# A fused attention and feed-forward kernel: one order of work exchanged for another, with the two banks of a PSUM tile counted as one

## The chip, the cores and the metric

The kernel runs on one core of a Trainium2 chip. The metric is device time in microseconds (us) of one execution. The core has five engines with instruction queues of their own: PE (matrix products), DVE and ACT and POOL (elementwise work), and SP, which here only issues DMA transfers. Each engine takes its instructions strictly in the order in which they are written; engines wait for one another through semaphores. Products land in PSUM, which has eight banks of 512 fp32 columns per partition.

## The reference

Eight batches of linear attention with a cosine weighting are followed by a feed-forward layer with leaky ReLU:

```python
def phi(x, c, s):
    r = np.maximum(x, 0.0)
    return np.concatenate([r * c, r * s], axis=-1)
q_p = phi(q, cos_w, sin_w)                     # q, k, v: (8, 8, 576, 64)
k_p = phi(k, cos_w, sin_w)
kv  = np.einsum('bhsf,bhsd->bhfd', k_p, v)
z   = np.sum(k_p, axis=2)
num = np.einsum('bhsf,bhfd->bhsd', q_p, kv)
den = np.einsum('bhsf,bhf->bhs', q_p, z)[..., None] + 1e-06
x = (num / den) as 4608 tokens x 512           # then:
h = x @ w_in                                   # 512 x 2048
g = np.maximum(0.01 * h, h)
out = g @ w_out                                # 2048 x 512
```

Inputs and output are fp32; the kernel computes in fp16 with fp32 sums.

## The kernel before

**Groups.** The 4608 tokens are nine groups of 512: group g < 8 is the first 512 tokens of batch g, group 8 the 64 last tokens of all eight batches. A number behind a step's name is its batch or group.

**Steps.** Loads are `Lq`, `Lk`, `Lv` (an ending a or b is half the heads, n the tail of 64 tokens), `Lw1`, `Lw2`; all go through SP's queue in their order, into four staging buffers that are used in turn (`stage`), so a load can start only when the casts that read the buffer's earlier content are done. `q1.0.c`, `k2.3.s` and the like are relu times cosine or sine into `qp` and `kp`; `cw2` casts a quarter of w_out (four quarters, two halves each: `cw2.2.0` is needed for hidden blocks 8 and 9 of 16). `K` sums kp times v into PSUM, `kv` copies it out; `T` (by PE, with copy `tc`) or `Tq` (by DMA) transposes q; `N` multiplies q with kv; `D` divides (three DVE instructions); `X` with `xc` (by PE) or `Tx` (by DMA) transposes the result into `xT`.

**Feed-forward.** Group 0 takes the plain route: `M` is its first product and `a` the leaky ReLU, `E` its second product (E3.7: hidden blocks 14 and 15 of 16, token quarter 3) and `ec` the copy out. Group 1's first product is `H` with `ha`. From then on products go as seven instead of eight block products with sums between: `P` is the first product of groups 2 to 8 and `F` the second of groups 1 to 8; `Ws`, `Xs`, `Tw`, `S` are the operand sums (DVE); `b s u y z` and `t r` the sums between products, `a c e d` the ReLUs; `st` stores.

**PSUM.** Eight banks are four pairs: `h0`, `h1`, `o`, `n`. The pair `n` is one tile of two banks for the whole kernel, `h0` and `h1` are one tile each until the step `split.h` (near F1.6) makes each two tiles, `o` is two tiles from the start. Semaphores are set by tile: a product that writes one bank of a tile waits for every reader of that tile that stands ahead of it in the order, and a reader on one engine waits for an earlier reader of the same tile on another. E2 and E3 use the two banks of `n`, as do the transposes X2.0 to X2.3 and every `N`.

**What sets the order.** Nothing in the file decides it: the string `ORDER` (from line 17 on) names some 1500 steps one after the other, with a letter for the engine where there is a choice (D is DVE, A is ACT, P is POOL), and the loop at the file's end issues them so. `idle` steps are PE products of zeros. In the order before, the second cast of w_out's third quarter stands on POOL, E3.7 stands behind the copy `ec2:D`, and the copies of X2 are `xc2.0:D xc2.1:A xc2.3:A xc2.2:D`.

Of the kernel before, what the change touches and what calls it, by code (L numbers as in the profile page):

```python
# [31 lines left out]
M10.1 kp1.0.c:D a5 q1.1.c:D M12.0 M4.1 M13.1 M12.1 q1.2.c:P M15.0 M15.1 M14.0 a2 a6 M14.1 cw2.1.1:D kp1.1.s:D
a7 E3.0 Lv1a k1b.8.c:D kp1.3.s:D E2.0 E1.0 cw2.1.0:A T1.0 Lk4n E0.0 E2.1 E1.1 E0.1 E2.2 tc1.0:A q1.2.s:A T1.1
kp1.2.s:D Lv1b q1.3.s:P E2.3 tc1.1:A k1b.5.c:A k1b.0.c:P E1.2 T1.2 v1.0:P tc1.2:D T1.3 E3.1 tc1.3:D k1b.6.c:D
k1b.1.c:P v1.1:A Lv2n K1a k1b.3.c:D Lw2.2 k1b.7.c:A kv1a:A k1b.2.c:D k1b.4.c:P E1.3 N1a.0 E0.2 Lw2.3 E3.2
N1a.1 D1a.0 v1.3:P D1a.1 v1.2:A E3.3 Lq2 K1b kv1b:D E0.3 cw2.2.0:P X1a.0 X1a.1 xc1a.1:D N1b.0 E1.4 xc1a.0:A
N1b.1 D1b.0 E2.4 E0.4 cw2.2.1:P X1b.0 Lk2n cw2.3.0:P xc1b.0:A D1b.1 E1.5 Tw1.0:D Tw2.0:D E0.5 Lk2 Ws1.1:D Lv2
X1b.1 xc1b.1:A H0.0 Ws1.2:D E2.5 H1.0 Ws0.2:D H2.0 H2.1 H3.0 E0.6 q2.1.c:D H1.1 H0.1 ha0 E3.4 q2.1.s:D E2.6
cw2.3.1:P H3.1 E2.7 H5.0 ha1 Tw3.0:D q2.0.s:A H5.1 E0.7 ec0:A H4.0 q2.0.c:A Ws1.4:D E1.6 H4.1 q2.2.s:P ha2
k2.4.s:D Lq3 q2.3.c:D st0.0 H6.0 q2.3.s:D E3.5 q2.2.c:P k2.0.s:A H7.0 Tw1.1:D H6.1 H7.1 H8.0 Tw2.1:D k2.3.s:P  # L40
# [11 lines left out]
k4.4.c:P P2.2.1 F1.4.0.0 N3.1 c2.1 b2.2:A P2.2.5 q4.0.s:A F1.4.0.1 P2.1.4 st0.2 s2.2:A D3.1 d2.1 S2.1l:D
q4.3.c:P F1.3.0.0 N3.2 P2.2.2 D3.2 st0.3 P2.2.6 F1.3.0.1 k4.0.c:P u2.2:A P2.2.3 P2.2.7 Lk5n F1.4.1.0 k4.2.s:D
k4.1.c:A q4.0.c:D Lq5 N3.3 k4.1.s:P a2.2 z2.2:D k4.3.s:A P2.3.1 D3.3 e2.2 F1.3.1.0 v4.0:P F1.3.1.1 v4.1:P
b2.3:A P2.3.5 P2.3.6 k4.3.c:A k4.2.c:A y2.2:D F1.4.1.1 u2.3:A k4.0.s:A st1.2 c2.2 P2.3.2 s2.3:D Tx3 r1.4:D
P2.2.4 r1.3:D P2.3.3 P2.3.7 K4 a2.3 d2.2 z2.3:D e2.3 y2.3:D P2.3.4 q4.2.c:P S2.2l:D F2.1.0.0 d2.3 F2.6.0.0
kv4:D F2.1.0.1 F2.1.1.0 F2.1.1.1 c2.3 S2.1h:D P3.0.1 k5.4.s:P Xs3.1:D Xs3.2:D b3.0:A Tq4.0 P3.0.5 Xs3.3:D
S2.2h:D Tq4.1 P3.1.1 S2.3l:D s3.0:A Xs3.4:D P3.0.6 u3.0:A t1.2:A P3.0.2 q5.3.s:P Lk5 q5.0.s:P F2.6.0.1 P3.0.7
F2.6.1.0 z3.0:D P3.0.3 a3.0 y3.0:D F2.6.1.1 N4.0 P3.1.5 F2.2.0.0 e3.0 b3.1:A P3.1.2 D4.0 t2.2:D st1.5 Lv5
q5.0.c:A S2.3h:D q5.1.c:A P3.1.6 N4.1 s3.1:A P3.0.4 Lv5n F2.2.0.1 Lq6 q5.2.s:P a3.1 F2.2.1.0 D4.1 d3.0 P3.1.3  # L60
P3.2.1 u3.1:A z3.1:D P3.2.5 F2.7.0.0 F2.7.0.1 e3.1 N4.2 q5.1.s:D P3.1.7 c3.0 F2.2.1.1 D4.2 b3.2:A y3.1:D
F2.7.1.0 st1.4 F2.7.1.1 S2.4l:D s3.2:A P3.2.6 P3.2.2 u3.2:D c3.1 t3.2:D P3.1.4 k5.2.s:P N4.3 k5.3.s:D P3.2.3
a3.2 P3.2.7 r2.2:A d3.1 z3.2:D k5.0.s:A F2.4.0.0 F2.4.0.1 F2.5.0.0 P3.3.5 y3.2:D k5.2.c:P e3.2 q5.3.c:P P3.3.1
k5.1.c:A D4.3 b3.3:A S2.4h:D P3.2.4 Tq5.0 Tx4 F2.5.0.1 P3.3.6 F2.5.1.0 s3.3:A q5.2.c:D k5.1.s:D F2.5.1.1 c3.2
k5.0.c:P F2.4.1.0 u3.3:A d3.2 P3.3.7 F2.4.1.1 r2.5:D P3.3.3 P3.3.2 v5.1:A v5.0:A k5.3.c:A F2.3.0.0 st1.3
k5.4.c:D F2.3.0.1 y3.3:D r2.4:D c3.3 P3.3.4 F2.3.1.0 F3.1.0.0 F2.3.1.1 z3.3:D e3.3 d3.3 K5 q6.0.s:D q6.1.c:D
Lk6 Lk6n a3.3 Lv6 S3.1h:D F3.1.0.1 P4.0.1 S3.1l:D b4.0:A Xs4.1:D S3.2l:D P4.1.1 P4.0.5 Xs4.2:D st2.5 S3.2h:D
kv5:A P4.0.6 Xs4.3:D Xs4.4:D u4.0:A r2.3:D P4.0.2 s4.0:A a4.0 F3.1.1.0 P4.0.7 N5.0 S3.3h:D P4.0.3 F3.6.0.0
z4.0:D F3.6.0.1 e4.0 st2.2 P4.1.5 F3.1.1.1 q6.0.c:D k6.4.s:P F3.6.1.0 b4.1:A Tq5.1 y4.0:D F3.6.1.1 s4.1:A
t1.3:A D5.0 P4.1.6 u4.1:A st2.4 P4.1.3 N5.1 P4.0.4 P4.1.7 F3.2.0.0 S3.3l:D t2.3:D c4.0 z4.1:D d4.0 F3.2.0.1  # L70
q6.1.s:A D5.1 y4.1:D k6.0.s:P k6.2.c:D F3.2.1.0 P4.1.2 k6.0.c:A F3.7.0.0 P4.2.1 F3.2.1.1 Lv6n e4.1 a4.1 P4.2.5
F3.7.0.1 b4.2:D r3.2:D s4.2:A P4.2.6 P4.2.2 k6.2.s:P S3.4h:D P4.1.4 k6.4.c:A q6.2.c:P q6.3.s:D q6.2.s:P
F3.5.0.0 u4.2:D N5.2 F3.7.1.0 q6.3.c:P k6.3.c:A D5.2 d4.1 c4.1 a4.2 Lq7 F3.7.1.1 Tq6.0 F3.5.0.1 P4.3.1 v6.1:A
N5.3 P4.2.7 t3.3:D F3.5.1.0 F3.4.0.0 z4.2:D v6.0:A D5.3 P4.2.3 Tx5 Lv7n P4.3.5 y4.2:D F3.4.0.1 k6.1.c:D
k6.1.s:A e4.2 F3.5.1.1 Lk7n st2.3 F3.4.1.0 b4.3:A P4.3.6 k6.3.s:D c4.2 s4.3:D P4.2.4 u4.3:A F3.4.1.1 S3.4l:D
P4.3.7 r3.5:D S4.1l:D K6 d4.2 y4.3:D q7.0.c:P P4.3.2 S4.2l:D F3.3.0.0 kv6:A P4.3.4 z4.3:D Xs5.1:D c4.3 N6.0
P4.3.3 Xs5.3:D Xs5.2:D d4.3 Tq6.1 F3.3.0.1 Lk7 e4.3 F3.3.1.0 r3.4:D P5.0.1 P5.1.1 q7.1.c:P a4.3 Lt0.0 P5.0.5
F3.3.1.1 b5.0:D s5.0:A D6.0 P5.0.6 P5.0.2 P5.0.3 F4.1.0.0 q7.0.s:A st3.2 r3.3:D S4.1h:D N6.1 u5.0:A P5.0.7
a5.0 Xs5.4:D S4.2h:D P5.1.5 z5.0:D y5.0:D F4.1.0.1 e5.0 k7.4.s:P k7.4.c:A F4.1.1.0 F4.6.0.0 b5.1:D F4.6.0.1
k7.1.c:P s5.1:A Lv7 q7.1.s:D F4.6.1.0 P5.0.4 P5.1.2 P5.1.6 c5.0 q7.3.s:D P5.1.3 D6.1 F4.1.1.1 q7.3.c:D  # L80
F4.6.1.1 d5.0 u5.1:A a5.1 t1.4:A z5.1:D P5.1.7 S4.3l:D P5.2.1 F4.2.0.0 Tq7.0 st3.5 P5.2.5 y5.1:D N6.2 F4.2.0.1
F4.2.1.0 t2.4:D e5.1 F4.2.1.1 P5.1.4 F4.7.0.0 b5.2:A D6.2 k7.3.c:A s5.2:D P5.2.6 q7.2.s:A S4.3h:D N6.3 Lt0.1
r4.2:A P5.2.2 P5.2.3 F4.5.0.0 u5.2:A d5.1 k7.2.s:D a5.2 F4.7.0.1 z5.2:D P5.3.1 e5.2 b5.3:A F4.7.1.0 st3.4
P5.2.7 D6.3 c5.1 F4.7.1.1 st3.3 F4.5.0.1 k7.1.s:D k7.0.s:A y5.2:D Tx6 t3.4:D P5.3.5 k7.0.c:A P5.3.6 P5.3.2
S4.4l:D v7.1:D q7.2.c:D k7.2.c:A u5.3:A s5.3:D k7.3.s:A F4.5.1.0 F4.4.0.0 c5.2 v7.0:P P5.2.4 z5.3:D F4.5.1.1
d5.2 Lt1.0 K7 r4.5:D S4.4h:D P5.3.7 Xs6.1:D P5.3.3 y5.3:D Xs6.3:D F4.3.0.0 a5.3 Xs6.2:D F4.4.0.1 F4.4.1.0
# [894 lines left out]
```

## Time and profile before

| | |
|---|---|
| median of 3 runs | 275.84 us (275.52 to 275.86) |
| the profiled execution's own time | 275.22 us |
| its span, from first to last instruction | 273.4 us |
| PE / PE's weight loads busy | 264.4 / 223.9 us |
| DVE / ACT / POOL busy | 215.2 / 179.3 / 104.4 us |
| HBM read / written | 36.70 / 9.44 MB |
| TensorE clock granted | 0.996 |

A row of the profile's timeline has the start, the duration, the engine, the line in the file, the operation with its output and inputs (buffer numbers left out), how many instructions are merged in it, and in brackets how long the engine sat idle before it and what it waited for. A product's duration in these rows (0.59 us for a first one of 512 columns) is longer than the distance to the next one, since products are pipelined; the distance is what counts for PE's time.

### The profile page before, as it was taken

Reading aid. Unit: us, or ns where it says so; the run is one execution under the profiler, and the core shown is the slowest. Engines: PE = TensorE matmul, PEld = TensorE weight load, DVE = VectorE, ACT = ScalarE, POOL = GpSimd, SP = SyncE. Lnnn points to the kernel's source line nnn. Section 1 sums busy time; section 2 is a strip of 40 time slices with the busy share of each in tenths; the row PEclk is TensorE's granted clock in tenths of the full one; section 3 lists DMA queues with packets and bytes.
Section 4 is the critical chain, followed back from the end, with each engine's and each line's share of the span. In section 5 each row is a group of like instructions: output and inputs, shape, how many; then the busy total and the mean of one; then the engine's idle time right before and its main releaser. Section 6 shows DMA issues by size and latency. Waiting matters only on the chain.

```text
span 273.4 us, 6788 instructions
## 1 busy us (share of the span) xinstructions
PE 264.4 (97%) x2734; PEld 223.9 (82%) x2734; DVE 215.2 (79%) x429; ACT 179.3 (66%) x306; POOL 104.4 (38%) x76
## 2 busy tenths in 40 slices
...
GB/s 236 357 395 384 400 330 353 344 267 272 319 187 349 218 178 262 345 187 260 262 200 168 168 336 207 154 191 78 120 63 131 80 93 61 40 79 0 41 134 97
DMA packets 87631, 57.06 MB, mean 209 GB/s; under 512 B 53808, under 2 KB 82480, under 8 KB 87088
## 3 DMA queue, kind: packets, MB, share of 16 engines
...
q10 hardware_dynamic: 608, 0.52, 0.6%
...
HBM read 36.70 MB, written 9.44 MB: 169 GB/s over the span
## 4 chain that ended last, share of the span: by engine, by line
PE 82%; DMA 10%; DVE 4%; SPq 1%; issue 1%; ACT 1%; POOL 0%; ACTq 0%
PE o L869 32%; PE h L783 32%; DMA stage<-in_moe_w_out_dram 7%; PE h L685 5%; PE n L558 3%; PE n L470 3%; DMA stage<-in_k_dram 2%; PE n L707 1%; PE o L707 1%; PE h L869 1%; PE n L869 1%; DVE xs L582 1%; DVE kp L431 1%; SPq L321 1%; PE o L374 0%
## 5 line engine op out<-in xcount | busy, mean ns | idle before, releaser
L869 PEld LDWEIGHTS <-g 128*128 128x128 f16 x640 | 61.8, 98 | 6.5
L869 PE MATMUL o<-w,g 128*128 128x256 f16 x480 | 64.7, 273 | 0.0
L803 ACT ACTIVATE g<-h 128x512 f16<-128x512 f32 x84 | 48.4, 600 | 24.0 <-PE h L783 12.7
L783 PEld LDWEIGHTS <-w 128*128 128x128 f16 x448 | 48.2, 114 | 1.4 <-issue 0.5
L783 PE MATMUL h<-xT,w 128*128 128x256 f16 x336 | 48.9, 273 | 0.3 <-ACT xT L234 0.3
L783 PEld LDWEIGHTS <-wext 128*128 128x128 f16 x336 | 36.5, 114 | 0.7 <-issue 0.2
L869 PE MATMUL o<-T,ext 128*128 128x256 f16 x224 | 31.6, 273 | 0.0
L242 POOL TENSOR_SCALAR qp<-stage,cos_t 128x512 f16<-128x512 f32 (+1 forms) x12 | 26.1, 2176 | 13.6 <-DMA stage<-in_q_dram 6.6
L242 POOL TENSOR_SCALAR kp<-stage,sin_t 128x512 f16<-128x512 f32 (+1 forms) x12 | 21.3, 1777 | 23.8 <-DMA stage<-in_k_dram 13.8
L869 PEld LDWEIGHTS <-ext 128*128 128x128 f16 x256 | 24.9, 98 | 2.6
L230 DVE TENSOR_TENSOR h<-h,u 128x512 f32<-128x512 f32 x28 | 19.5, 695 | 9.1 <-PE h L783 3.9
L783 PE MATMUL h<-X,wext 128*128 128x256 f16 x176 | 25.4, 272 | 0.0
L230 DVE TENSOR_TENSOR y<-h,s 128x512 f32<-128x512 f32 x28 | 19.2, 685 | 4.4 <-PE h L783 3.3
L242 POOL TENSOR_SCALAR kp<-stage,cos_t 128x128 f16<-128x128 f32 (+2 forms) x13 | 18.6, 1434 | 9.7 <-DMA stage<-in_k_dram 9.7
L582 DVE TENSOR_TENSOR xs<-n,rden 128x512 f16<-128x512 f32 x30 | 20.7, 692 | 1.0
L242 POOL TENSOR_SCALAR qp<-stage,sin_t 128x512 f16<-128x512 f32 (+1 forms) x9 | 19.1, 2126 | 6.2 <-DMA qpT<-qp 5.3
L234 ACT COPY h<-h 128x512 f32<-128x512 f32 x24 | 13.8, 574 | 9.9 <-PE h L783 9.5
L803 ACT ACTIVATE g<-y 128x512 f16<-128x512 f32 x28 | 17.7, 632 | 1.7 <-DVE y L230 1.7
L869 PE MATMUL o<-ext,g 128*128 128x256 f16 x128 | 18.2, 272 | 0.0
L230 DVE TENSOR_TENSOR osb<-o,ext 128x512 f32<-128x512 f32 x22 | 15.0, 686 | 2.5 <-PE o L869 1.7
L234 ACT COPY u<-h 128x512 f32<-128x512 f32 x21 | 12.3, 586 | 7.0 <-PE h L783 6.9
L783 PE MATMUL h<-X,w 128*128 128x256 f16 x112 | 16.9, 273 | 0.0
...
## 6 DMA issues: line engine op xcount, KB each, us to landing
...
```

Source lines behind the costliest of these rows:

```text
L230: eng.tensor_tensor(out=o, in0=a, in1=b, op=how)
L234: nc.scalar.copy(o, i)
L242: eng.tensor_scalar(out=o, in0=i, scalar1=0.0, scalar2=col, op0=ALU.max, op1=ALU.mult)
L321: nc.sync.dma_start(w2_st(i), w2v[i])
L470: nc.tensor.matmul(ps[:, h // NC, (h % NC) * NE : (h % NC + 1) * NE], lhsT=kps[sl, s, :], rhs=vms[sl, s, :], start=start, stop=stop, skip_ ...
L558: nc.tensor.matmul(pairs["n"][lo:hi, h // 4, (h % 4) * NE : (h % 4 + 1) * NE], lhsT=qpT[j // 2][:, j % 2, h, lo:hi], rhs=kv[b][:, h, :],)
L582: nc.vector.tensor_tensor(out=o, in0=ps[:, :, 0 : 4 * NE].rearrange("p a (b e) -> p a b e", e=NE)[:, :, :, 0:D], in1=r.rearrange("p (a b) ...
L685: nc.tensor.matmul(ps[:, m % 2], lhsT=w1[m // 4, c // 2][:, c % 2, m % 4 : 512 : 4], rhs=xT[1][:, :, c, :], start=(c == 0), stop=(c == NKC ...
L707: nc.tensor.matmul(bank[4 + tt], lhsT=G[0][:, m, tt * P : (tt + 1) * P], rhs=w2[:, m, :], start=(m == 0), stop=(m == NFT - 1),)
L783: nc.tensor.matmul(ps[:, mi * HT : (mi + 1) * HT], lhsT=a[:, c, 2 * r0 + mi : 512 : 4], rhs=b[:, c], start=(n in (1, 5) and mi == 0 and c ...
L803: nc.scalar.activation(G[g % 2][:, m : m + 2, r * HT : (r + 1) * HT], {"a": A, "c": y22, "e": E, "d": B_}[e].rearrange("p (m t) -> p m t", ...
L869: nc.tensor.matmul(ps[:, tt], lhsT=a[:, i, tt * P : (tt + 1) * P], rhs=b[:, i], start=(first and i == 0 and (apart or tt == 0)), stop=(i = ...
```

## The change

Only the string `ORDER` differs. Up to `M1.1.1 N0b.1 D0b.1 idle.5.1.5`, that is through the loads and attention of the first batch, it is the same; from there to the end the same steps stand in another order, and some on another engine (of the steps with a letter or a fixed engine, DVE has 357 in place of 352, ACT 293 in place of 301, POOL 68 in place of 65). The new order was made by a planner, which is not in the file, that treats the two banks of one PSUM tile as one resource. PE's instructions are the same in number and kind.

```diff
-M1.1.0 M1.1.1 N0b.1 D0b.1 idle.5.1.5 X0b.0 M2.0.0 M3.0.0 xc0b.0:A M3.0.1 M3.1.0 M2.0.1 Lq1 X0b.1 q1.0.s:D M5.0
+M1.1.0 M1.1.1 N0b.1 D0b.1 idle.5.1.5 M2.0.0 M2.0.1 M3.0.0 X0b.0 M3.0.1 xc0b.0:D M2.1.0 M2.1.1 M3.1.0 X0b.1
...
-E1.7 k2.2.s:A k2.2.c:D H9.0 Ws0.4:D H9.1 E3.6 H8.1 Tq2.1 k2.3.c:P ec2:D k2.4.c:D k2.1.c:D ec1:A ha3 k2.1.s:D
-E3.7 Tq2.0 k2.0.c:D H11.0 H10.0 H10.1 ha4 H11.1 H13.0 Lk3 S1.1l:D H12.0 S1.3l:D v2.0:D Ws0.3:D ha5 Tw4.1:D
+q2.2.s:D E3.5 q2.0.s:D q2.0.c:D q2.2.c:D E3.6 H0.1 H1.0 H1.1 H2.0 Tw2.0:D H2.1 ha0 Lq3 H3.0 H3.1 k2.3.c:D E3.7
+H4.0 q2.3.s:P Lv2 Ws0.2:D ec2:D k2.3.s:A Tw4.0:D k2.2.c:P Lv2n H4.1 ha1 H6.0 H5.0 Tq2.0 ec1:D H6.1 H5.1 ha2
...
-r1.2:A F1.7.0.0 N2.3 k3.0.c:P D2.3 st0.1 F1.7.0.1 F1.5.0.0 F1.7.1.0 S1.4l:D X2.1 Tq3.0 v3.0:D X2.0 Tq3.1
-k3.3.s:A X2.2 X2.3 v3.1:A xc2.0:D xc2.1:A xc2.3:A F1.5.0.1 k3.4.c:A F1.5.1.0 P2.0.1 F1.7.1.1 xc2.2:D b2.0:A
+F1.7.0.1 F1.7.1.0 q3.3.c:A X2.0 X2.1 Ws0.4:D r1.2:A X2.2 S1.4l:D X2.3 xc2.0:D xc2.1:D F1.5.0.0 v3.0:A Lk4
+xc2.2:D xc2.3:D Xs2.1:D F1.7.1.1 F1.5.0.1 k3.3.s:P k3.2.c:A v3.1:A P2.0.1 Xs2.2:D F1.5.1.0 b2.0:A F1.5.1.1
```

Three places show how the instructions move. First SP's queue around the loads of w_out's third and fourth quarter (`in_moe_w_out`; the loads of 64 partitions are the tails `Lk4n`, `Lv2n` and so on). Before:

```order
L321 DMA stage_78<-in_moe_w_out_dram 128x2048
L275 DMA stage_80<-in_k_dram 128x2x576
L275 DMA stage_77<-in_v_dram 128x2x576
L292 DMA stage_79<-in_k_dram 64x4x64 x2
L275 DMA stage_77<-in_v_dram 128x2x576
L292 DMA stage_78<-in_v_dram 64x4x64 x2
L321 DMA stage_78<-in_moe_w_out_dram 128x2048
L321 DMA stage_79<-in_moe_w_out_dram 128x2048
L269 DMA stage_80<-in_q_dram 128x8x256
```

Now:

```order
L321 DMA stage_78<-in_moe_w_out_dram 128x2048
L275 DMA stage_80<-in_k_dram 128x2x576
L275 DMA stage_77<-in_v_dram 128x2x576 x2
L321 DMA stage_78<-in_moe_w_out_dram 128x2048
L321 DMA stage_79<-in_moe_w_out_dram 128x2048
L292 DMA stage_79<-in_k_dram 64x4x64 x2
L269 DMA stage_80<-in_q_dram 128x8x256
L292 DMA stage_77<-in_k_dram 64x4x64 x2
L285 DMA stage_77<-in_k_dram 128x8x256
```

The two tail loads that stood ahead of the third quarter, and between the halves of v1, now stand behind the fourth quarter (Lk4n) and far behind (Lv2n).

Second DVE's queue around `ec2`, the copy `osb<-n` (L236) that E3.7 stood behind; `T` and `wext` are weight sums, `qp` and `kp` the relu products of batch 2. Before:

```order
L230 TENSOR_TENSOR T_112<-w_111 128x1024
L230 TENSOR_TENSOR T_113<-w_111,T_112 128x1024
L242 TENSOR_SCALAR kp<-stage_77,cos_t 128x8x64
L230 TENSOR_TENSOR wext<-w_0_1_104,wext 128x1024
L236 COPY osb<-n_76 128x512
L242 TENSOR_SCALAR kp<-stage_77,cos_t 128x4x64
L242 TENSOR_SCALAR kp<-stage_77,cos_t 128x8x64
L242 TENSOR_SCALAR kp<-stage_77,sin_t 128x8x64
L242 TENSOR_SCALAR kp<-stage_77,cos_t 128x8x64
L230 TENSOR_TENSOR ext<-g_101 128x1024
```

Now:

```order
L230 TENSOR_TENSOR T_113<-w_111,T_112 128x1024
L242 TENSOR_SCALAR kp<-stage_77,cos_t 128x8x64
L230 TENSOR_TENSOR wext<-wext,w_0_0_103 128x1024
L236 COPY osb<-n_76 128x512
L230 TENSOR_TENSOR ext<-w_111,T_113 128x1024
L236 COPY osb<-o_64 128x512
L236 COPY osb<-n_76 128x512
L242 TENSOR_SCALAR kp<-stage_77,sin_t 128x8x64
L230 TENSOR_TENSOR w_1_0_105<-w_0_0_103,w_1_0_105 128x1024
L242 TENSOR_SCALAR kp<-stage_77,cos_t 128x4x64
```

The copy stands earlier in DVE's queue than before, and E3.7 now stands ahead of it in the whole order; all of ec1, ec2 and ec3 are DVE's (ec1 and ec3 were ACT's), and the weight sum Tw4.0 (`ext<-w,T`) stands between ec2 and ec1.

Third DVE's queue at the transposes of group 2: `xs<-n` is the last instruction of a division, `xT<-n` a copy `xc2`. Before, with two of the four copies on ACT:

```order
L582 TENSOR_TENSOR xs<-n_76,rden_126 128x512
L230 TENSOR_TENSOR g_101<-g_101,ext 128x4x256
L236 CAST vm<-stage_77 128x18x64
L236 COPY xT_98<-n_76 128x512 x2
L230 TENSOR_TENSOR X_114<-xT_98 128x512
L230 TENSOR_TENSOR X_115<-xT_98,X_114 128x512
```

Now, with all four on DVE:

```order
L582 TENSOR_TENSOR xs<-n_76,rden_126 128x512
L230 TENSOR_TENSOR wext<-w_0_1_104,wext 128x1024
L230 TENSOR_TENSOR g_101<-g_101,ext 128x4x256
L236 COPY xT_98<-n_76 128x512 x4
L230 TENSOR_TENSOR X_114<-xT_98 128x512
L230 TENSOR_TENSOR X_115<-xT_98,X_114 128x512
```

The cast of v3 (L236 `vm<-stage`) left this place for ACT, the weight sum Ws0.4 came into it, and the four copies stand together.

More of the change, by code (lines that the diff above doesn't have):

```diff
@@ L32 @@
[L32 to L40, printed above, removed]
-E1.7 k2.2.s:A k2.2.c:D H9.0 Ws0.4:D H9.1 E3.6 H8.1 Tq2.1 k2.3.c:P ec2:D k2.4.c:D k2.1.c:D ec1:A ha3 k2.1.s:D
@@ L52 @@
[L52 to L86, printed above, removed]
```

126 lines of the change are left out of this document (85 added, 41 removed).

## The prediction

> **What bounds the kernel now.** I read the page's busy times, then a table by stretches, then PE's timeline where PE has gaps.
>
> ```profile
> span 273.4 us, 6788 instructions
> PE 264.4 (97%) x2734; PEld 223.9 (82%) x2734; DVE 215.2 (79%) x429; ACT 179.3 (66%) x306; POOL 104.4 (38%) x76
> ```
>
> PE sets the time, but 97% is no measure of what can be won, since products overlap in these rows. The table by stretches (columns: stretch, then PE, PEld, DVE, ACT, POOL busy with counts, clock, DMA share, GB/s) says where room is:
>
> ```profile
> 48.00:56.00 8.00, 8.00 (x39) 3.97 (x37) 7.93 (x13) 4.25 (x6) 7.09 (x5) 1.00 1.10 345
> 56.00:64.00 8.00, 7.65 (x37) 3.84 (x35) 5.82 (x11) 5.36 (x8) 4.54 (x3) 1.00 1.13 232
> 64.00:72.00 8.00, 7.64 (x99) 5.87 (x98) 7.86 (x15) 7.77 (x13) 6.61 (x4) 1.00 1.12 330
> 72.00:80.00 8.00, 7.67 (x87) 6.68 (x86) 6.41 (x15) 5.95 (x11) 3.77 (x2) 1.00 1.18 231
> 88.00:256.00 168.00, 168.00 (x1803) 158.37 (x1802) 140.41 (x278) 117.77 (x212) 44.94 (x25) 1.00 0.68 160
> ```
>
> ```profile
> L558 PE MATMUL n<-kv,qpT 128*128 128x66 f16 (+1 forms) x216 | 9.7, 195 | 0.0
> L470 PE MATMUL n<-vm,kp 128*128 128x66 f16 (+1 forms) x160 | 5.7, 193 | 0.0
> ```
>
> From 88 us on PE has no gap. Of its 1803 products there 376 are of 66 columns (the two groups just shown, from the view by lines), 1427 of 256. A product of 256 columns takes 0.109 us from start to start (0.87 for eight in the rows below, less the overlap), one of 66 takes 0.031: 155.5 + 11.7 = 167.2 of 168. In 168 us, 0.8 are lost, and no order wins more there. Where the new order differs and PE has gaps is 18 to 81 us, and the timeline of PE shows them:
>
> ```profile
> 18.35 0.71 PE L661 MATMUL h<-xT,w 128*128 128x256 f16 x5
> 19.15 0.40 PE L594 MATMUL o<-ident,xs 128*128 128x128 f16 x4
> 43.49 0.42 PE L569 MATMUL h<-kv,qpT 128*128 128x66 f16 x8
> 44.27 0.59 PE L707 MATMUL o<-w,g 128*128 128x512 f16 x2 [0.36 <-POOL w L236]
> 59.73 0.59 PE L685 MATMUL h<-xT,w 128*128 128x512 f16 x2
> 60.67 0.59 PE L707 MATMUL n<-w,g 128*128 128x512 f16 x2 [0.35 <-DVE osb L236]
> 61.10 5.34 PE L685 MATMUL h<-xT,w 128*128 128x512 f16 x24
> 69.64 1.04 PE L869 MATMUL o<-T,ext 128*128 128x256 f16 x8
> 71.03 0.41 PE L558 MATMUL n<-kv,qpT 128*128 128x66 f16 x8 [0.36 <-DVE xs L582]
> 72.16 0.60 PE L869 MATMUL o<-w,g 128*128 128x256 f16 x4
> 72.79 0.41 PE L558 MATMUL n<-kv,qpT 128*128 128x66 f16 x8
> 77.32 1.04 PE L869 MATMUL o<-T,ext 128*128 128x256 f16 x8
> 78.65 0.60 PE L783 MATMUL h<-xT,w 128*128 128x256 f16 x4 [0.29 <-ACT xT L234]
> 81.04 1.15 PE L470 MATMUL n<-vm,kp 128*128 128x66 f16 x31
> ```
>
> The loss is the next start less the last start plus the products' distances (24 of 512 columns in 5.34 give 0.216 each): at 19.15 it is 0.25; at E1.4 44.27 - (43.49 + 8 x 0.031) = 0.53; at E3.7 60.67 - (59.73 + 0.43) = 0.51; at N2.1 71.03 - (69.64 + 0.87) = 0.52; at N2.2 0.19; at P2.0.1 78.65 - (77.32 + 0.87) = 0.46. These six are 2.46 us, and the whole room is little more. The last row is K3, behind which both orders have done the same products.
>
> **The change, place by place.** PE's work is the same, so the sum is over its waits.
>
> *18 to 43 us, the first products M and the first E.* M2.0.0, M2.0.1 and M3.0.0 now stand ahead of X0b.0. M2 writes h0 and must wait for the same division as X0b.0 did, so they don't fill that wait; but with two more quarter products ahead of X0b.1 its wait of 0.25 falls by 0.22. M6.0 then stands only 1.1 us of products behind the last one that the ReLU a0 needs:
>
> ```profile
> L670 ACT ACTIVATE g<-h 128x1024 f16<-128x1024 f32 x7 | 7.2, 1025 | 4.9 <-PE h L661 4.9
> L431 DVE SCALAR_TENSOR_TENSOR kp<-stage,sin_t x4: 744/746/747, 33.1 to 37.4; 128x576 f16<-128x576 f32 x4
> ```
>
> a0 takes 1.03 and starts some 0.2 behind its product's start, so M6.0 waits about 0.2: even. Later N1a.0 stands behind tc1.3, and DVE has one kp step of 0.75 and a small one between tc1.2 and tc1.3, so N1a.0 may wait 0.2 to 0.5, while one product of E more is done by then (0.43). I take 0 for the stretch, bounds 0.4 either way.
>
> *E1.4.* It waits for the cast of w_out's third quarter, which waits for the load:
>
> ```profile
> 35.91 7.21 DMA stage<-in_moe_w_out_dram
> 43.18 1.05 POOL w L236
> 32.19 1.33 SPq L292 DMA_DIRECT2D stage<-in_k_dram  x2
> 34.20 1.26 SPq L292 DMA_DIRECT2D stage<-in_v_dram  x2
> DMA packets 3579, 6.13 MB, mean 361 GB/s; under 512 B 1460, under 2 KB 2424, under 8 KB 3214
> ```
>
> The first two are the chain of waits, then two rows of SP's queue, then the DMA view from 31 to 47 us, where the engines are full. The change takes the two tail loads away from in front, four pieces of 64 KB: 256 KB at 361 GB/s are 0.7 us, and if their small packets count by SP's issue time, up to 1.3 + 1.3. I take 1.4. The cast is then done at about 42.8 in place of 44.2, and by PE's work E1.4 is due at about 43.1. Bounds of the gain: 0.1 (0.7 alone, with four short products less ahead of E1.4) to 0.5. I take 0.4.
>
> *E3.7.* It writes one bank of n and waits for the copy of E2 from the other:
>
> ```profile
> 59.93 0.69 DVE L236 COPY osb<-n 128x512 f32<-128x512 f32 x1 [2.14 <-PE n L707]
> ```
>
> Now E3.7 stands ahead of that copy: 0.51 goes. DVE was idle 2.14 us before it, so nothing else held it. The Trainium skill's page "PSUM — Partial Sum Buffer" (section Specifications (TRN2)) says that ScalarE and VectorE reach PSUM in parallel at full rate as long as they don't collide in a bank; by that rule banks 6 and 7 need no wait on each other and there would be nothing to win here, 1.1 in the sum below. The row has PE start 0.05 after the copy's end, so the wait is the program's, by tile, and the trace decides.
>
> *K2 and DVE.* What is won at E1.4 and E3.7 lasts only if K2 (which needs v2.0, a cast on DVE) isn't late. DVE's rows from the last division of batch 1 to that cast:
>
> ```profile
> 46.36 1.03 DVE L230 TENSOR_TENSOR T<-w 128x1024 f16<-128x1024 f16 x1
> 47.42 1.41 DVE L230 TENSOR_TENSOR T<-w,T 128x1024 f16<-128x1024 f16 x1
> 51.49 0.90 DVE L242 TENSOR_SCALAR qp<-stage,sin_t 128x512 f16<-128x512 f32 x1
> 54.61 0.47 DVE L242 TENSOR_SCALAR qp<-stage,sin_t 128x512 f16<-128x512 f32 x1
> 55.01 0.68 DVE L230 TENSOR_TENSOR T<-w 128x1024 f16<-128x1024 f16 x1
> 63.67 0.75 DVE L236 CAST vm<-stage 128x1152 f16<-128x1152 f32 x1
> ```
>
> These are the first and the last of 24, with some between: 46.36 to 64.42 less 2.14 idle, 15.9 us. In the new order there are 24 again, with three sums of 1024 (0.68 to 1.41) less, two copies of 0.69 and one cast of 0.75 more: about 15.4. They start when D1b.1 ends, 0.2 + 1.1 behind N1b.1, so the cast ends 16.7 to 16.8 us behind N1b.1. PE has 41 steps from there to K2, 40 of two 0.216 products and one short: 17.5 us. K2 is clear by 0.7; I take 0.
>
> *N2.1 and N2.2.* Each waits for a division of the step before, on DVE, and DVE is full (7.86 of 8). Ahead of D2.0 DVE now has six steps behind v2.0 in place of eight: at 0.6 to 0.7 each about 1.3 less, while K2 comes about 0.9 earlier. So D2.0 starts 0.3 to 0.4 nearer to PE's work: N2.1's 0.52 becomes about 0.2. N2.2 keeps its 0.2; N2.3, which had no wait, gets about 0.1, as three F steps stand ahead of it in place of four. Gain 0.2, bounds -0.3 to 0.6.
>
> *P2.0.1.* The copies of X2 go over one tile, and DVE and ACT take turns:
>
> ```profile
> 77.56 0.42 DVE L236 COPY xT<-n 128x512 f16<-128x512 f16 x1
> 79.12 0.42 DVE L236 COPY xT<-n 128x512 f16<-128x512 f16 x1 [1.14 <-ACT xT L234]
> ```
>
> With four copies of 0.42 on DVE, two are done 0.8 behind the first start, and the cast of 0.75 ahead of them is gone (a sum of 0.68 is there). PE has F1.5.0.0, F1.7.1.1 and F1.5.0.1, 1.3 us, behind the transposes to cover them. I take 0.4 of 0.46, plus 0.1 at the next product. Bounds 0.1 to 0.6.
>
> *From 81 us on* the new order has waits that I can't tell one by one; the old one lost 0.8, so at most 0.8 is won; I take 0 and let it lose as much.
>
> *Sum:* 0 + 0.4 + 0.51 + 0 + 0.2 + 0.5 = 1.6 us. The execution's 275.22 (1.8 around its span of 273.4) becomes 273.6, and the median, 0.6 higher, 275.84 - 1.6 = 274.2.
>
> **The rivals.**
>
> *Given back on DVE (0.20).* Where DVE sets the pace from 64 to 80 us, PE arrives earlier and waits longer. For it: 7.86 of 8 busy, and two of the six gaps end with DVE's `xs`. Against: eight steps ahead of D2.0 become six. Then only P2.0.1's 0.5 stays: 275.3.
>
> *Slower: v2.0 late for K2 (0.12).* One mechanism: sums and casts on DVE stretch beside POOL. The rows have 1.03 and 1.41 against 0.68, and 0.90 against 0.47. If half of nine sums (+0.38) and eight casts (+0.43) stretch, 15.4 gets 3.4 longer, K2 is 2.7 late, and only 1.6 of it is paid by the gains: 275.84 - 1.6 + 2.7 = 276.9. It decides from a chain of about 17.7 us on (0.7 of slack and 1.6 of gain used up). Against: the same mixture took 15.9 with POOL 7.09 of 8 busy from 48 to 56. The Trainium skill's "GPSIMD Engine Reference" (section 1, Specifications) says that GpSimd shares its SBUF interfaces with VectorE and collides with instructions of two SBUF inputs. By that rule all nine sums would stretch; the trace has sums of 0.68 amid POOL's work, so it agrees in part.
>
> *The order only moves waits (0.10).* The new order was made without a clock from the chip as far as the profile tells; if K4's inputs on POOL cost what the early places win, the time stays at 275.8.
>
> ```profile
> L242 POOL TENSOR_SCALAR kp<-stage,sin_t 128x512 f16<-128x512 f32 (+1 forms) x12 | 21.3, 1777 | 23.8 <-DMA stage<-in_k_dram 13.8
> ```
>
> Eight such steps, three of them short, now stand on POOL between K3 and K4, some 13 us, and PE has 17 us of products there: clear by about 2 us, if batch 4's load isn't late.
>
> **How the numbers follow.** The forecast, 274.2, has 0.58; its own range from the bounds is 273.2 to 275.1. About 0.2% (0.55 us) is what a measurement here can tell. Faster: 0.58 and two fifths of "given back", 0.66. Same: the other three fifths and most of "only moves waits", 0.19. Slower: 0.12 and the rest, 0.15. The range for 8 in 10 goes from 272.9 (all bounds at their best, and some of the 0.8) to 276.1, into the rivals.
>
> **What would show it.** Right: E1.4 with less than 0.2 of loss, E3.7 with none, the four `xT<-n` copies in a row on DVE and P2.0.1 at about 76.7; K3 some 1.5 to 2 us before its 81.0; from there a constant lead. Wrong: a gap of PE at K2 that ends with `vm` on DVE; N2.1's gap grown by what was won before; a wait of K4 on POOL; PE's gaps behind 88 us above 1.5 us in all.

## The result and the profile after

The new order takes 273.11 us (median of 6 runs, 272.54 to 273.56), the old one beside it 275.61 (275.18 to 275.86). The ratio is 0.9907, with a 95% interval of 0.9891 to 0.9923: 2.6 us less, between 2.1 and 3.0. The forecast was 274.2, that is 1.6 less, in a range of 272.9 to 276.1. In 11 of the 30 runs of three variants below (the loads put back, the copies put back, the first of the two cut orders) the granted clock was 0.989 to 0.994 in place of 0.995 to 1.0, and in the median they took 1.4 to 1.8 us longer.

The page of the new order, and the view of PE's waits (columns: line, what was waited for, us in all, times, longest):

```profile
span 270.8 us, 6779 instructions
PE 263.8 (97%) x2734; PEld 224.0 (83%) x2734; DVE 215.9 (80%) x434; ACT 175.9 (65%) x298; POOL 117.3 (43%) x79
```

```profile
PE o L374 <- DVE osb L409: 1.2, 1, 1.2
PE o L537 <- POOL qp L242: 0.8, 1, 0.8
PE h L661 <- ACT kv L234: 0.2, 1, 0.2
```

All three stand in the head that both orders share. The waits for `w` on POOL, `osb` and `xs` on DVE and `xT` on ACT, which the prediction quoted, are gone. PE's timeline at the same places:

```profile
41.94 0.74 PE L458 MATMUL h<-vm,kp 64*128 64x66 f16 x36
42.62 1.04 PE L707 MATMUL o<-w,g 128*128 128x512 f16 x4
...
52.67 1.03 PE L685 MATMUL h<-xT,w 128*128 128x512 f16 x4
53.53 0.59 PE L707 MATMUL n<-w,g 128*128 128x512 f16 x2
...
62.81 2.10 PE L685 MATMUL h<-xT,w 128*128 128x512 f16 x9
64.75 1.41 PE L470 MATMUL n<-vm,kp 128*128 128x66 f16 x40
...
68.11 1.04 PE L869 MATMUL o<-T,ext 128*128 128x256 f16 x8
68.99 0.42 PE L558 MATMUL n<-kv,qpT 128*128 128x66 f16 x8
...
70.11 0.60 PE L869 MATMUL o<-w,g 128*128 128x256 f16 x4
70.62 0.42 PE L558 MATMUL n<-kv,qpT 128*128 128x66 f16 x8
...
75.66 0.60 PE L869 MATMUL o<-T,ext 128*128 128x256 f16 x4
76.10 0.60 PE L783 MATMUL h<-xT,w 128*128 128x256 f16 x4
...
78.28 1.41 PE L470 MATMUL n<-vm,kp 128*128 128x66 f16 x40
```

Read as before, next start less last start less the products' distances: E1.4 (42.62) follows K1b without a gap, E3.7 53.53 - 52.67 - 4 x 0.216 = 0, K2 64.75 - 62.81 - 9 x 0.216 = 0, N2.1 68.99 - 68.11 - 0.87 = 0.01, N2.2 0.07, P2.0.1 76.10 - 75.66 - 0.44 = 0. K3 starts at 78.28 in place of 81.04. On DVE v2.0, the cast for K2, and the four copies, which stand in a row:

```profile
62.46 0.75 DVE L236 CAST vm<-stage 128x1152 f16<-128x1152 f32 x1
...
75.06 1.41 DVE L236 COPY xT<-n 128x512 f16<-128x512 f16 x4
```

From K3 to the end not all of its 2.76 us stays. DVE's last sum, of the old order and of the new:

```profile
268.75 0.42 DVE L230 TENSOR_TENSOR stage<-h,ext 128x256 f32<-128x256 f32 x1 [0.38 <-PE h L869]
```

```profile
266.43 0.42 DVE L230 TENSOR_TENSOR stage<-h,ext 128x256 f32<-128x256 f32 x1 [0.45 <-PE h L869]
```

It is 2.32 earlier, so 0.44 is given back between K3 and it; and from it to the end of the span it is 4.65 us before and 4.37 now, 0.28 less. 2.76 - 0.44 + 0.28 = 2.6, the difference of the spans (273.4 and 270.8). Of this, 0.25 comes from ahead of the place where the orders part, and is chance: the first instruction that differs starts at 17.86 us in this profile, and the one at its place in the old order's at 18.11. Over the fourteen profiles of this document, which all share that head, it is 17.82 to 18.53; in two variants of the new order below it is 18.37 and 18.43.

### The profile page after: what moved, and what is told of

Read it like the earlier page. It is cut to its first block, busy times and chain, and to the rows that moved or that the text cites. A ratio compares the mean times of both kernels' runs of the same rounds, so it can differ in the third digit from the quotient of the medians.

```text
span 270.8 us, 6779 instructions
## 1 busy us (share of the span) xinstructions
PE 263.8 (97%) x2734; PEld 224.0 (83%) x2734; DVE 215.9 (80%) x434; ACT 175.9 (65%) x298; POOL 117.3 (43%) x79
## 4 chain that ended last, share of the span: by engine, by line
PE 86%; DMA 6%; DVE 3%; POOL 1%; SPq 1%; issue 1%; ACT 1%; DVEq 0%; POOLq 0%
PE o L869 33%; PE h L783 31%; PE h L685 5%; DMA stage<-in_moe_w_out_dram 5%; PE n L558 3%; PE n L470 3%; PE n L707 2%; PE o L707 2%; DMA stage<-in_q_dram 2%; PE h L869 1%; PE n L869 1%; DVE xs L582 1%; PE h L458 1%; POOL qp L242 1%; PE o L374 1%; PE h L569 1%
## 5 line engine op out<-in xcount | busy, mean ns | idle before, releaser
L869 PE MATMUL o<-w,g 128*128 128x256 f16 x480 | 65.7, 273 | 0.0
L242 POOL TENSOR_SCALAR qp<-stage,cos_t 128x512 f16<-128x512 f32 (+1 forms) x14 | 30.3, 2164 | 36.2 <-DMA qpT<-qp 20.8
L242 POOL TENSOR_SCALAR kp<-stage,cos_t 128x128 f16<-128x128 f32 (+2 forms) x17 | 27.1, 1597 | 17.6 <-DMA stage<-in_k_dram 17.6
L242 POOL TENSOR_SCALAR kp<-stage,sin_t 128x512 f16<-128x512 f32 (+1 forms) x15 | 28.3, 1894 | 5.9 <-PE n L470 5.2
L783 PE MATMUL h<-X,wext 128*128 128x256 f16 x176 | 26.2, 273 | 0.1
L234 ACT COPY u<-h 128x512 f32<-128x512 f32 x24 | 14.1, 589 | 9.5 <-PE h L783 9.5
L242 POOL TENSOR_SCALAR qp<-stage,sin_t 128x512 f16<-128x512 f32 (+1 forms) x8 | 17.5, 2195 | 6.0 <-DVE rden L581 2.9
L234 ACT COPY h<-h 128x512 f32<-128x512 f32 x23 | 13.2, 574 | 6.9 <-PE h L783 6.4
L783 PE MATMUL h<-xT,wext 128*128 128x256 f16 x112 | 16.8, 273 | 0.0
```

Of the source, the lines that this page charges most:

```text
L234: nc.scalar.copy(o, i)
L242: eng.tensor_scalar(out=o, in0=i, scalar1=0.0, scalar2=col, op0=ALU.max, op1=ALU.mult)
L783: nc.tensor.matmul(ps[:, mi * HT : (mi + 1) * HT], lhsT=a[:, c, 2 * r0 + mi : 512 : 4], rhs=b[:, c], start=(n in (1, 5) and mi == 0 and c ...
L869: nc.tensor.matmul(ps[:, tt], lhsT=a[:, i, tt * P : (tt + 1) * P], rhs=b[:, i], start=(first and i == 0 and (apart or tt == 0)), stop=(i = ...
```

## Experiments

Times are given against runs of the old order on the same chip (275.5), worked out from the ratio. Gaps of PE are reckoned as in the prediction.

### E3.7 alone, in the old order

```diff
-E3.6 H8.1 Tq2.1 k2.3.c:P ec2:D k2.4.c:D k2.1.c:D ec1:A ha3 k2.1.s:D E3.7 Tq2.0
+E3.6 H8.1 Tq2.1 k2.3.c:P E3.7 ec2:D k2.4.c:D k2.1.c:D ec1:A ha3 k2.1.s:D Tq2.0
```

> The old order with one step moved: E3.7 is issued ahead of the copy ec2, so that it need not wait for it; PE's own order stays. Theory 1 (the waits are separate, as the prediction's sum took them): PE's wait of 0.51 us at E3.7 goes and nothing else changes, 0.5 under the kernel before, about 275.1. Theory 2 (VectorE sets the pace from ec2 to the divisions of batch 2: in the trace of before it works from 59.93 to 74.4 us with no idle time over 0.1): ec2 now waits for E3.7 to end and starts at about 60.7 in place of 59.93, the whole row of VectorE's steps behind it is late by 0.7 to 0.9, and PE's wait at N2.1 grows from 0.5 to 1.7 or more: 0.3 to 0.9 over the kernel before, 275.9 to 276.5, in spite of the wait removed.

Measured: 276.69, ratio 1.0035 (1.0022 to 1.0047): 1.0 us slower. First DVE, then PE:

```profile
61.28 0.69 DVE L234 COPY osb<-n 128x512 f32<-128x512 f32 x1 [3.71 <-PE n L705]
```

```profile
60.65 0.59 PE L705 MATMUL n<-w,g 128*128 128x512 f16 x2
...
71.57 0.61 PE L867 MATMUL o<-T,ext 128*128 128x256 f16 x4 [1.13 <-DVE ext L228]
72.60 0.41 PE L556 MATMUL n<-kv,qpT 128*128 128x66 f16 x8 [0.42 <-DVE xs L580]
```

E3.7 (60.65) starts 0.43 behind the product ahead of it, without a gap, and the copy now ends 1.35 later than the 59.93 + 0.69 of before, as it waits for E3.7. All that stands behind it on DVE is late, and PE waits 1.13 for a sum and 0.42 for the division of N2.1. The second theory holds: in the old order DVE sets the pace from ec2 to the divisions of batch 2, and curing PE's wait at E3.7 at the price of a later ec2 wins nothing.

The same with E3.7 one product earlier and two sums out of DVE's way:

```diff
-E3.6 H8.1 Tq2.1 k2.3.c:P ec2:D
+E3.6 E3.7 H8.1 Tq2.1 k2.3.c:P ec2:D
...
+K3 Tw4.1:D Ws1.3:D
```

> The old order with E3.7 issued right behind E3.6 and ahead of ec2, as in e37_ahead (one product earlier), and with two weight sums of VectorE, Tw4.1 and Ws1.3 (0.68 us each), taken from between ec2 and batch 2's divisions and put behind K3. Theory (the wait at E3.7 and VectorE's row of steps behind ec2 have to be cured together): ec2 starts about 0.45 us later than before, the two sums give back 1.3, so the division that N2.1 waits for ends some 0.8 earlier than in the kernel before, while PE arrives 0.5 earlier: E3.7 without wait, N2.1 with 0 to 0.3 in place of 0.5; 0.5 to 0.9 us under the kernel before, about 274.8, unless the two sums make VectorE late behind K3 (then about even). Rival (what e37_ahead lost is not VectorE's row but the earlier product itself): as slow as e37_ahead, 0.5 or more over the kernel before.

Measured: 275.73, ratio 1.0005 (0.9991 to 1.0019), no difference. PE's timeline:

```profile
69.09 1.04 PE L867 MATMUL o<-T,ext 128*128 128x256 f16 x8
69.97 0.42 PE L556 MATMUL n<-kv,qpT 128*128 128x66 f16 x8
...
79.86 1.42 PE L468 MATMUL n<-vm,kp 128*128 128x66 f16 x40
...
83.01 0.60 PE L781 MATMUL h<-xT,wext 128*128 128x256 f16 x4 [0.74 <-DVE h L228]
```

N2.1 has no wait (69.97 - 69.09 - 0.87 = 0.01) and K3 starts at 79.86, 1.2 ahead of the old order. Behind K3 the two sums delay DVE, PE waits 0.74 there, and the lead at DVE's last sum is down to 0.3 (268.46) in this execution, the shortest of the twelve (274.89). So the two waits have to be cured together, and the work that is put off has to find room.

### The tile of two banks as two tiles, in the old order

No step is moved. `split.n` and `join.n` close the pool of `n` and open it with two tiles or with one:

```diff
+    op("split.n", change, ("n",), 2)
+    op("join.n", change, ("n",), 1)
...
-cw2.1.1:D kp1.1.s:D a7 E3.0
+cw2.1.1:D kp1.1.s:D a7 split.n E3.0
...
-H13.1 ec3:A v2.1:A
+H13.1 ec3:A join.n v2.1:A
```

> The old order with the pair of banks n opened as two tiles of one bank from ahead of the first product E2 or E3 until ec3, and as one tile of two banks again from there; no step is moved. If two engines may be in the two banks at one time (the wait of E3.7 is made by the tile alone), PE's wait at E3.7 (0.51 us) goes, ec2 no longer waits for the products E3 and starts up to 2.1 us earlier, VectorE's row of steps behind it moves ahead and PE's wait at N2.1 shrinks too: 0.5 to 1.2 us under the kernel before, 274.4 to 275.1. If the banks of a pair disturb each other, the wait goes but the products E3 beside the copy or the copy itself (0.69 us) take longer, and the time stays within 0.3 of the kernel before.

Measured: 274.52, ratio 0.9958 (0.9945 to 0.9971): 1.2 us faster.

```profile
57.72 0.68 DVE L235 COPY osb<-n 128x512 f32<-128x512 f32 x1
```

```profile
59.83 0.59 PE L684 MATMUL h<-xT,w 128*128 128x512 f16 x2
60.26 0.59 PE L706 MATMUL n<-w,g 128*128 128x512 f16 x2
...
69.23 1.04 PE L868 MATMUL o<-T,ext 128*128 128x256 f16 x8
70.10 0.42 PE L557 MATMUL n<-kv,qpT 128*128 128x66 f16 x8
```

E3.7 and N2.1 have no gap, and ec2 starts 2.21 earlier, without idle time ahead of it. The two waits of 0.51 and 0.52 are thus made by the one tile, and both fall with it. At 57.72 to 58.40 PE writes no product of `n` (the nearest are at 55.94 and 59.40), so whether a copy and a product in the two banks disturb each other isn't shown here.

### The loads, in the old order and in the new

```diff
-T1.0 Lk4n E0.0
+T1.0 E0.0
...
-v1.1:A Lv2n K1a k1b.3.c:D Lw2.2
+v1.1:A K1a k1b.3.c:D Lw2.2
...
-E0.2 Lw2.3 E3.2
+E0.2 Lw2.3 Lk4n Lv2n E3.2
```

> The old order with only the two tail loads Lk4n and Lv2n moved in SP's queue, from ahead of w_out's third quarter to behind its fourth. Prediction's term: the cast for E1.4 is done 0.7 to 1.4 us earlier, E1.4's loss of 0.53 falls below 0.2, and as VectorE waits for PE ahead of ec2 (2.14 us idle) nothing behind it takes that back: 0.3 to 0.5 us under the kernel before, about 275.1. Rival (the casts on POOL set E1.4, not the load): the load lands earlier, the gap stays, the same time as before.

Measured: 275.02, ratio 0.9977 (0.9967 to 0.9988): 0.6 us faster. The time is as the prediction's term wants it, but the profile doesn't show the gain where the term had it. So it was profiled once more:

> The same kernel as loads_behind, profiled once more. In its profile E1.4 had no wait, but N1b.1 waited 0.45 us for a copy on ScalarE, VectorE's row ahead of it was 0.55 late behind one step of kp that took 1.23 in place of 0.75 us, and the span ended 3.9 us behind the start of the last sum in place of 4.65. If these come from the order, they are here again: the kp step over 1.1 us, PE's E1.4 to N1b.1 worth nothing (X1b.1 at 47.5), and 3.9 to 4.0 us from the last sum to the end. If they are chance, at least one of them is away, and X1b.1 is at 46.6 to 47.1.

Measured: 274.81 in its one run. All three were there again. PE, DVE and POOL of this second profile:

```profile
44.23 0.59 PE L705 MATMUL o<-w,g 128*128 128x512 f16 x2
45.27 0.42 PE L567 MATMUL h<-kv,qpT 128*128 128x66 f16 x8 [0.45 <-ACT xT L232]
```

```profile
36.74 1.90 DVE L429 SCALAR_TENSOR_TENSOR kp<-stage,sin_t 128x576 f16<-128x576 f32 x2
```

```profile
38.02 1.90 POOL L240 TENSOR_SCALAR kp<-stage,cos_t 128x128 f16<-128x128 f32 x2
41.16 2.03 POOL L234 CAST w<-stage 128x1024 f16<-128x1024 f32 x2 [0.59 <-DMA stage<-in_moe_w_out_dram]
```

and of the old order:

```profile
36.74 1.42 DVE L431 SCALAR_TENSOR_TENSOR kp<-stage,sin_t 128x576 f16<-128x576 f32 x2
```

```profile
38.67 1.57 POOL L242 TENSOR_SCALAR kp<-stage,cos_t 128x128 f16<-128x128 f32 x2
```

The cast starts 2.0 us earlier (41.16 for 43.18) and E1.4 no longer waits. But v1's first half lands earlier too, POOL goes to its kp step at 38.02, beside DVE's second one there, and the two DVE steps take 1.90 in place of 1.42. The attention of batch 1 is then 0.5 late (K1a starts at 39.30 in place of 38.81), and N1b.1 waits 0.45 for a copy of it. X1b.1 starts at 47.48, in the old order at 46.99: on PE the change has won nothing. What makes it faster is the end:

```profile
269.10 0.42 DVE L228 TENSOR_TENSOR stage<-h,ext 128x256 f32<-128x256 f32 x1 [0.38 <-PE h L867]
```

The span is 273.0 here, so 3.9 us from the last sum to the end, in place of 4.65. The last sum is later and the end is earlier.

Now the two loads put back ahead of the third quarter in the new order:

```diff
-E1.2 E0.2 Lw2.2 E0.3
+E1.2 E0.2 Lk4n Lv2n Lw2.2 E0.3
```

> The new order with only the two tail loads Lk4n and Lv2n put back ahead of w_out's third quarter. Taking them away in the old order made the cast start 1.95 us earlier (43.18 to 41.23). Theory (in the new order nothing else waits there, so E1.4 pays in full): the cast is done 0.7 to 1.95 us later than 42.16, E1.4, due at 42.62, waits 0.3 to 1.5 and nothing takes it back: 0.3 to 1.5 us over the new kernel. Rival (a wait at E1.4 is covered by one behind it, as in loads_behind): the wait is there, and the time is within 0.2 of the new kernel.

Measured: 275.58, ratio to the old order 1.0012 (0.999 to 1.0034): the gain of the change is gone, about 2.5 us over the new order.

```profile
43.67 1.38 POOL L234 CAST w<-stage 128x1024 f16<-128x1024 f32 x1 [2.78 <-DMA stage<-in_moe_w_out_dram]
```

```profile
45.10 1.02 PE L705 MATMUL o<-w,g 128*128 128x512 f16 x4 [2.11 <-POOL w L234]
```

E1.4 is 2.48 later than in the new order, more than the bound of 1.5, and nothing behind it takes that back. The cast itself is 2.5 late (43.67; in the new order 41.13). DVE's last sum is at 269.05, 2.6 behind the new order's. So E1.4 follows the load in both orders. In the old one the copy that N1b.1 waits for ended at 44.73 and N1b.1 started at 44.79, right behind E1.4, so another wait stood under E1.4's; in the new one eight steps E, from E1.4 to E1.6, stand ahead of N1b.1, and PE doesn't wait there.

### The copies xc2, in the old order and in the new

```diff
-v3.1:A xc2.0:D xc2.1:A xc2.3:A F1.5.0.1 k3.4.c:A F1.5.1.0 P2.0.1 F1.7.1.1 xc2.2:D b2.0:A
+v3.1:A xc2.0:D xc2.1:D xc2.2:D xc2.3:D F1.5.0.1 k3.4.c:A F1.5.1.0 P2.0.1 F1.7.1.1 b2.0:A
```

> The old order with only the four copies xc2 changed: all on VectorE, one behind the other, in place of VectorE, ScalarE, ScalarE, VectorE. Prediction's term: P2.0.1 loses under 0.15 in place of 0.46 and the wait ahead of P2.0.5 stays at 0.2: 0.3 to 0.45 us under the kernel before, about 275.15. Rival (VectorE, which has 0.75 of casting right ahead of the copies here, then is late with the sums X for P2.0.5 and P2.0.6, and gives it back): the time of before within 0.15.

Measured: 274.91, ratio 0.9979 (0.9969 to 0.999): 0.6 us faster.

```profile
77.31 1.04 PE L867 MATMUL o<-T,ext 128*128 128x256 f16 x8
78.36 0.63 PE L781 MATMUL h<-xT,w 128*128 128x256 f16 x4
```

P2.0.1 loses 78.36 - 77.31 - 0.87 = 0.18 in place of 0.46 (under 0.15 was expected), and K3, at 80.57, is 0.47 earlier: the term holds, at its upper bound.

In the new order, with the engines of before:

```diff
-xc2.0:D xc2.1:D F1.5.0.0 v3.0:A Lk4 xc2.2:D xc2.3:D Xs2.1:D
+xc2.0:D xc2.1:A xc2.3:A F1.5.0.0 v3.0:A Lk4 xc2.2:D Xs2.1:D
```

> The new order with only the copies xc2 as before: xc2.1 and xc2.3 on ScalarE, between VectorE's xc2.0 and xc2.2. The prediction's term (the engines' turns over one tile make the wait): P2.0.1 waits 0.3 to 0.45 again, 0.3 to 0.45 us over the new kernel. Rival (the order of PE and VectorE around it makes the difference: VectorE begins the copies at 75.06 with P2.0.1 due at 76.10, one us of cover, in place of 0.6 before): xc2.1 ends at about 76.05, P2.0.1 waits under 0.1, the sums X are 0.5 later but not waited for more than 0.2: within 0.25 of the new kernel.

Measured: 275.54, ratio to the old order 1.0012 (0.9993 to 1.0031): about 2.4 over the new order. Both theories are wrong in size. ACT, then PE:

```profile
75.76 1.07 ACT L232 COPY xT<-n 128x512 f16<-128x512 f16 x2 [1.74 <-DVE xT L234]
...
79.44 0.59 ACT L232 COPY h<-h 128x512 f32<-128x512 f32 x1
```

```profile
76.39 0.60 PE L781 MATMUL h<-xT,w 128*128 128x256 f16 x4
...
80.08 0.60 PE L781 MATMUL h<-X,wext 128*128 128x256 f16 x4 [1.68 <-DVE xT L228]
```

P2.0.1 (76.39) doesn't wait, as the rival said. But ACT sits idle 1.74 for its turn at the tile, and behind the two copies stand two casts of v3, a kp step and b2.0 (the copy `h<-h`). b2.0 ends at 80.03, and P2.0.6, which needs its bank, starts at 80.08. The view names DVE's `xT`, which ended at 80.07 by chance; in the program P2.0.6 waits for b2.0 and for a sum that ended at 78.20. PE loses 80.08 - 77.80 - 0.44 = 1.84 there, the larger part of the 2.4; where the rest lies is not settled.

### v2.0 behind three more steps, in the new order

```diff
-H13.0 v2.0:D ha5
+H13.0 Ws1.4:D q3.1.c:D Tw3.1:D v2.0:D ha5
```

> The new order with the cast v2.0 put behind three more steps of VectorE, Ws1.4, q3.1.c and Tw3.1 (0.68, 0.83 and 0.68 us), which stood right behind it: the rival in which v2.0 is late for K2, made on purpose. In the new kernel v2.0 ends at 63.20 and K2 starts at 64.75, 1.55 later. Theory (this is slack, and beyond it each us is paid): v2.0 ends at about 65.2, K2 waits 0.4 to 0.6, and the time is 0.3 to 0.6 over the new kernel. Rival (the slack is shared with what follows, since VectorE feeds batch 2's divisions too): the wait comes again at N2.1, 1 us or more over the new kernel. If v2.0 has no part in it: no change.

Measured: 273.42, 0.3 over the new order's 273.11; the ratio to the old order, 0.9933 (0.9915 to 0.9951), overlaps with the new order's.

```profile
64.42 0.75 DVE L234 CAST vm<-stage 128x1152 f16<-128x1152 f32 x1
```

```profile
61.64 3.62 PE L683 MATMUL h<-xT,w 128*128 128x512 f16 x16
65.22 1.41 PE L468 MATMUL n<-vm,kp 128*128 128x66 f16 x40
```

The cast ends at 65.17 and K2 starts at 65.22, with a loss of 65.22 - 61.64 - 16 x 0.216 = 0.12. The slack was about 1.5 us, and the three steps (1.6, as q3.1.c took 0.48) use it up; no wait came at N2.1. Beyond the edge it wasn't pushed.

### Three edits together in the old order

n as two tiles, the loads behind and the copies xc2 on DVE, as above.

> The old order with n as two tiles from E2 to ec3, the two tail loads behind w_out's fourth quarter and the four copies xc2 on VectorE. If the three add up: 1.0 (n_two_tiles alone) + 0.4 + 0.35 = 1.7 to 1.8 us under the kernel before, about 273.8, that is within 0.7 of the new order as a whole. If VectorE or ScalarE then become the bound of this stretch: 1.0 to 1.2 under, no better than n_two_tiles alone.

Measured: 273.65, ratio 0.9929 (0.9913 to 0.9945): 2.0 us faster, against 1.2 + 0.6 + 0.6 = 2.4 of the three alone. In its profile the wait at N1b.1 is there as in loads_behind, N2.1 has none, and from the last sum (267.73) to the end it is 4.0 us. The last sum is thus 1.0 earlier than in the old order, where the new order has 2.3, and the other 0.7 of this profile's 1.7 come behind it. In time the three make up most of the whole change's 2.6, but up to the last sum less than half of it, and nothing here beats the new order.

### The orders cut at K3

Up to K3 by one order, and the steps that are then left in the other's sequence:

```diff
 s2.0:D P2.0.6 k3.1.s:A u2.0:A K3
-kv3:A P2.0.2 a2.0 Xs2.3:D z2.0:D k4.4.s:P P2.0.7 P2.0.3 Tw4.1:D
+Tw4.1:D Ws1.3:D Lq4 Tq3.1 S1.4h:D Xs2.3:D Lv4 z2.0:D r1.5:D P2.0.2 P2.0.7 kv3:A a2.0 P2.0.3
```

> The new order up to and with K3, and behind it the steps that are left in the old order's sequence. Theory (the gain is made ahead of K3, and the new tail loses a little): K3 starts at about 78.3 us as in the new kernel (81.0 before), and the new kernel's loss behind K3 (PE's start of the last product moves by 0.37 us less than K3 does) is not paid: 2.5 to 2.8 us under the kernel before, 272.8 to 273.1. Rival (the lead at K3 is only kept if the later steps were planned for it): 0.5 to 1.5 us of it are given back in waits of PE between 78 and 130 us, 273.5 to 274.5.

Measured: 278.1, ratio 1.0091 (1.0064 to 1.0119): 2.5 us slower than the old order. PE's waits, then DVE:

```profile
PE n L556 <- DVE xs L580: 2.0, 1, 2.0
...
PE h L781 <- DVE xT L228: 1.0, 1, 1.0
```

```profile
79.17 0.68 DVE L228 TENSOR_TENSOR ext<-w,T 128x1024 f16<-128x1024 f16 x1
...
80.98 0.61 DVE L228 TENSOR_TENSOR xT<-xT 128x512 f16<-128x512 f16 x1
...
87.45 0.49 DVE L240 TENSOR_SCALAR qp<-stage,sin_t 128x512 f16<-128x512 f32 x1 [3.24 <-DMA qpT<-qp]
```

Both expectations missed it. The new order reaches K3 early partly because it has put off four sums of DVE, two loads and a transpose by DMA that the old order has done by then. In the old sequence all of them come at once: the sums from 79.17 on (P2.0.7 waits 1.0 for the last), and a step on `qp` that waits 3.24 for the late transpose, which delays the division that N3.1 waits 2.0 for. Behind that wait the granted clock falls to a half from 89.90 to 93.31, and PE loses another 1.7 (half of 3.41): four products of 256 columns, 0.60 elsewhere, take 1.06 at 90.39 and at 91.25. The page's row of the clock shows it in its fourteenth slice:

```profile
PEclk9999999999999799999999999999999999999998
```

The two of its six runs with a clock of 0.999 and 1.0 took 277.39 and 276.81. So this order is 1.3 to 1.9 us slower than the old one at full clock, and the rest of the 2.5 goes with the clock. Whether the wait makes the clock fall is not shown: the wait of 2.11 at E1.4, with the loads put back, is followed by no such fall in its profile.

The other way round, the old order up to K3 and then the new sequence:

> The old order up to and with K3, and behind it the steps that are left in the new order's sequence. Theory: K3 at 81.0 us as before, and the new tail costs 0 to 0.4 us: the kernel before's time plus 0 to 0.4, 275.6 to 276.1. Rival (part of the gain sits in the new tail): 0.5 us or more under the kernel before.

Measured: 276.54, ratio 1.004 (1.0023 to 1.0056): 1.1 us slower, which is more than the 0 to 0.4 expected; K3 is at 81.32 and DVE's last sum at 270.26, 1.5 later than in the old order. Up to K3 the order is the old one, so the 0.28 there is chance: E1.4 loses 1.10 in this profile, and 0.48 to 0.64 in the five others that begin with the old order's loads. The other 1.2 is lost behind K3. No part of the gain sits in the new tail by itself, and neither tail suits the other's beginning.

## Why the prediction was right, and where its sizes were off

*18 to 43 us, 0 taken.* K1b starts at 41.94, and at 41.92 before, but by then the new order has done one step E more (E0.3, 0.43). At equal work PE leads by 0.41: 0.25 is the chance ahead of 17.86, and 0.16 is won in the stretch, inside the bound of 0.4. X0b.1's loss fell from 0.25 to 0.05, as the step said. N1a.0's feared 0.2 to 0.5 did not come: tc1.3 and the kp step ahead of it were done in time.

*E1.4, 0.4 taken.* Measured 0.53, at the upper bound of 0.5; as the same beginning loses 0.48 to 1.10 over six profiles, its size is in part chance. But the price of the two loads was mis-sized: 1.4 taken, 2.0 (loads_behind) and 2.5 us (new_loads_back) measured in the cast's start. And the term stands only with N1b.1's new place: alone in the old order it wins nothing on PE. The step didn't look at the wait under E1.4's, so that the term came in full is luck.

*E3.7, 0.51 taken.* Measured 0.51. The reading that the wait is the program's, by tile, is shown by n_two_tiles. But as a cause of its own it was misread: taken away alone by the order of steps, it costs 1.0. The 2.14 of DVE's idle time ahead of ec2 was no free room either: the same tile held ec2, which starts 2.21 earlier with two tiles. What the sum put beside it as a separate small term, DVE's row from ec2 on, is as large (0.6, under N2.1 and N2.2). The new order itself was not run with E3.7 back behind ec2, so how the two share the gain there is argued from the old order.

*K2, 0 taken.* No wait. The slack was 1.5 in place of 0.7; DVE's 15.4 us came as 14.6 (48.60 to 63.20), and K2 started 1.5 behind v2.0's end. The slower rival, v2.0 late, didn't happen, and new_v2_late shows K2 as its place and about 1.5 us as the edge.

*N2.1 and N2.2, 0.2 taken.* This term was mis-sized: N2.1 went from 0.52 to 0.01, N2.2 from 0.19 to 0.07, 0.6 in all. The step set two steps less (1.3) against K2's lead of 0.9, as if DVE reached v2.0 no earlier than before. It does: v2.0 starts at 62.46 in place of 63.67. D2.0 begins 2.4 earlier and PE arrives 1.5 earlier, so PE no longer waits. "Given back on DVE" falls for the new order, and is what happened in e37_ahead.

*P2.0.1, 0.4 and 0.1 taken.* Measured 0.67 up to K3 (0.46, and 0.2 at the products behind it). In the old order the turns of the two engines are its cause (xc2_on_dve). In the new order the term's mechanism is not what the copies on ACT cost: with them P2.0.1 doesn't wait (new_xc2_back), and the wait is P2.0.6's, through ACT's row.

*From 81 us on, 0 taken.* Measured -0.44, inside the 0.8 allowed. No wait of K4 on POOL came. Which waits make it up is not settled: the largest single gap is 0.23 at 92.27, and the rest is spread thin. From the last sum to the end 0.28 was won, a term that the sum didn't have.

Measured, the terms give 0.4 + 0.5 + 0.5 + 0.6 + 0.7 - 0.4 + 0.3 = 2.6 in place of 1.6, and 0.25 of it is chance. So the forecast was right in its direction, in its places and within the wide range, and too small in its sum: 273.11 lies just under its own range of 273.2 to 275.1. The upper end of that range doesn't follow from the bounds either: at their worst, -0.4 + 0.1 + 0.51 - 0.3 + 0.1, nothing is won, which is 275.8. "The order only moves waits" falls: the waits are gone, and only 0.44 comes back.
